# Splitting the large weight and cache loads of a decode kernel between two issuing engines, by partition halves

## The chip, the cores and the metric

The kernel runs on one core of a Trainium2 chip. The time is the device time of one execution, in microseconds (us). The kernel before took 382.42 us, the median of three runs (380.34, 382.51, 382.42).

## What is computed

One decoding step for two sequences: a layer norm, then the sum of the input, a sliding-window attention over a key and value cache, and a gated bilinear feed-forward block. All data are float32.

```python
x: (2, 1, 512); k_cache, v_cache: (2, 32, 8192, 128); wq: (512, 4096); wo: (4096, 512)
w_gate, w_up: (512, 1376); w_down: (1376, 512)

def _A_ref(x, k_cache, v_cache, wq, wo):
    W = min(4096, max(256, Sk // 4))          # 2048 of the 8192 positions
    q = (x @ wq).reshape(B, Sq, 32, 128).transpose(0, 2, 1, 3)
    k, v = k_cache[:, :, Sk - W:, :], v_cache[:, :, Sk - W:, :]
    scores = jnp.einsum("bhqd,bhkd->bhqk", q, k) * (128 ** -0.5)
    o = jnp.einsum("bhqk,bhkd->bhqd", softmax(scores), v)
    return o.transpose(0, 2, 1, 3).reshape(B, Sq, 4096) @ wo

def _B_ref(x, w_gate, w_up, w_down):
    return ((x @ w_gate) * (x @ w_up)) @ w_down

xn = layernorm(x)
out = x + _A_ref(xn, ...) + _B_ref(xn, ...)
```

There is one query row for each sequence and head, so every element of the cache window and of the weights is used a few times and then never again. The kernel has to read 159.5 MB from memory.

## The kernel before

**The stream.** The host lays all weights and the cache window out in one array, `stream`, in the order in which the kernel uses them. `blocks()` lists the loads: each is a list of fields, such as `("k", h, CK)` for the keys of head h, and lands as 128 rows, one for each partition, with the fields side by side in the row. `UNIT` is 4608 floats, 18 KB a partition: a head's keys with a piece of `wq`, or a head's values with its piece of `wo`. `STEP` is three units, 54 KB a partition, the size of one buffer.

**The loads in order.** 256 KB (the first piece of `wq`, into a tile of its own), 3072 KB (keys of head 0), 6400 KB (half of gate and up, keys of head 1), 3712 KB, 4608 KB, sixteen of 6912 KB (three units each, so by turns keys-values-keys and values-keys-values), 6400 KB, 6656 KB, 4352 KB, and then ten small ones for the last values and `w_down`. A small tile with the input `x` is loaded by ACT at the start.

**Who issues them.** `pump()` issues a load as soon as one of the `BUFS = 3` buffers of 54 KB a partition is free. It is called once at the start and then from `done()`, which a step calls when it has used a field: when the last field of a buffer is used, the buffer is given back and `pump()` puts the next load's DMA into the program at that place. All of them go to SP's queue. The wait for the buffer's last readers (the reduction of a head's products on DVE, or the projection on PE) sits on the issuing instruction, so SP waits and nothing is behind it but the next load.

**Order.** PE, DVE, ACT and SP are wrapped in `InOrder`: what the code calls on an engine runs on it in the order of the calls. Every instruction recorded through the wrapper has line 85. GpSimd (POOL) is not wrapped; a scheduler decides the order of its instructions, which are the two all-reduces over partitions of each head (L277 `mm`, the maximum, and L289 `sum`).

**A head.** `products(h)` multiplies the keys by the query on DVE (`step<-step,q`), `sums(h)` reduces them over the head dimension (`s<-step`). `weights(h)` takes the maximum (DVE `m`, POOL `mm`, ACT `nm`) and the exponentials (ACT `p`, POOL `sum`). `reciprocals(h - 1)` on DVE follows behind it. The values of a head come `LAG = 3` heads later: `pv` on PE (`o_ps`), `copy_out` on ACT (`o_sb`), `transpose` on PE (`tr`) and ACT (`oT`), `project_o` on PE (`acc`). `project_q` on PE makes the queries of later heads (`q<-step,xnb`).

Of the kernel before, what the change touches and what calls it, by code (L numbers as in the profile page):

```python
# [16 lines left out]
P = 128  # L17
# [15 lines left out]
UNIT = CK + max(CP, CO)  # L33
# [67 lines left out]
def kernel(  # L101
# [8 lines left out]
    pe, dve, act, sp = (InOrder(tc, e) for e in (nc.tensor, nc.vector, nc.scalar, nc.sync))  # L110
# [23 lines left out]
    tiles, used, left, got = {}, {}, {}, {}  # L134
# [4 lines left out]
    def pump():  # L139
        nonlocal held  # L140
        while todo:
            key, fields, at = todo[0]
            if key not in tiles:
                if key[0] == "q":
                    tiles[key] = const.tile([P, NC * DH], F32, name="wq0")
                elif held == BUFS:
                    return
                else:
                    held += 1
                    tiles[key] = steps.tile([P, STEP], F32, name="step")  # L150
                used[key] = 0
            todo.pop(0)
            c0 = used[key]
            for kind, i, w in fields:
                got[kind, i] = (tiles[key][:, used[key] : used[key] + w], key)
                used[key] += w
            c1 = used[key]
            if at is None:
                sp.dma_start(tiles[key][:FR, c0:c1], wd_rest)
            else:  # L160
                src = stream[at : at + P * (c1 - c0)].rearrange("(p i) -> p i", p=P)
                sp.dma_start(tiles[key][:, c0:c1], src)

    def done(kind, i):
        nonlocal held
        _, key = got.pop((kind, i))
        left[key] -= 1
        if left[key] == 0 and key[0] != "q":
            del tiles[key]
            held -= 1  # L170
            pump()

    pump()

    mean_w = const.tile([P, P], F32, name="mean_w")
# [353 lines left out]
```

## Time and profile before

| | |
|---|---|
| median of 3 runs | 382.42 us (380.34 to 382.51) |
| the profiled execution | 380.73 us, of which its span is 378.9 us |
| PE, busy | 260.9 us (69%) |
| DVE, busy | 293.9 us (78%) |
| ACT, busy | 63.8 us (17%) |
| POOL, busy | 25.2 us (7%) |
| moved by DMA | 159.71 MB, mean 421 GB/s over the span |
| mean granted TensorE clock | 0.797 |

A group of instructions is written as line, engine, operation, output<-input; `x31` is how often it ran. An engine followed by q (SPq, ACTq) is the queue in which it issues its DMAs. In the table of DMA queues, q1 holds the loads that SP issues and q10 those that ACT issues; both are served by the same 16 DMA engines.

### The profile page before, as it was taken

To read this page: it belongs to the slowest core of one execution; us is meant where nothing else is said; L and a number is where in the kernel's file an instruction comes from. 1 tells how busy PE (TensorE), PEld (TensorE's weight loads), DVE (VectorE), ACT (ScalarE), POOL (GpSimd) and SP (SyncE) were. 2 spreads that over 40 slices of the span, in tenths; PEclk is the share of its full clock that TensorE was granted. 3 is DMA by queue.
4 is the path that set the end of the run, shared out by engine and by line. 5 is a ranking of instruction groups with operands and counts; after the bars stand their busy time and mean duration, and the time that the engine had idled before them with its cause. 6 is when DMAs were issued, how large, how long until landed. Compare 5 with 4: busy or idle time off the path is not lost.

```text
span 378.9 us, 3009 instructions
## 1 busy us (share of the span) xinstructions
PE 260.9 (69%) x1156; PEld 90.2 (24%) x1156; DVE 293.9 (78%) x142; ACT 63.8 (17%) x264; POOL 25.2 (7%) x75
## 2 busy tenths in 40 slices
PE   3919882867838675783876668388566848719996
PEld 3502221212303221221222123122122312202442
DVE  3739892996799499589949949994994998699920
ACT  1020020102112110210111121011112112212221
POOL 0000000000000000000000000010000000000000
PEclk9968986667888796887969698667968776855999
DMA  8999999999999999999999999999999999999993
GB/s 316 463 419 435 428 444 455 403 444 461 394 444 449 403 455 409 434 461 403 444 457 391 449 455 387 461 415 432 455 414 434 455 417 433 423 427 412 421 415 143
DMA packets 4893, 159.71 MB, mean 421 GB/s; under 512 B 552, under 2 KB 688, under 8 KB 1296
## 3 DMA queue, kind: packets, MB, share of 16 engines
q1 hardware_dynamic: 4728, 159.45, 97.9%
q8 instruction: 9, 0.15, 0.2%
q10 hardware_dynamic: 152, 0.08, 0.1%
q14 instruction: 4, 0.03, 0.0%
HBM read 159.52 MB, written 0.00 MB: 421 GB/s over the span
## 4 chain that ended last, share of the span: by engine, by line
DMA 55%; DVE 24%; PE 16%; ACT 3%; issue 1%; SPq 0%; POOL 0%; DVEq 0%
DMA step<-in_stream_dram 55%; DVE s L85 12%; DVE step L85 12%; PE o_ps L85 6%; PE q L85 4%; PE acc L85 3%; PE tr L85 3%; ACT o_sb L85 1%; ACT oT L85 1%; ACT p L85 1%; DVE m L85 0%; SPq L85 0%; POOL mm L277 0%; DVE rec L85 0%; DVE o_sb L85 0%
## 5 line engine op out<-in xcount | busy, mean ns | idle before, releaser
L85 DVE TENSOR_TENSOR step<-step,q 128x4096 f32<-128x4096 f32 x31 | 136.6, 4407 | 57.2 <-DMA step<-in_stream_dram 57.2
L85 DVE TENSOR_REDUCE s<-step 128x32 f32<-128x4096 f32 x32 | 141.4, 4420 | 1.1
L85 PE MATMUL q<-step,xnb 128*128 128x512 f32 (+1 forms) x128 | 89.8, 847 | 59.4 <-DMA step<-in_stream_dram 59.2
L85 PE MATMUL o_ps<-step,p 128*8 128x512 f32 x512 | 87.7, 723 | 8.4 <-DMA step<-in_stream_dram 7.5
L85 PEld LDWEIGHTS q<-step,xnb 128*128 128x128 f32 x128 | 30.9, 265 | 113.4 <-DMA step<-in_stream_dram 56.9
L85 PE MATMUL tr<-x_t,o_sb 128*128 128x2 f32 x256 | 34.3, 256 | 25.1 <-ACT o_sb L85 24.7
L85 PE MATMUL acc<-step,oT 128*2 128x512 f32 (+1 forms) x76 | 41.1, 659 | 13.1 <-ACT oT L85 13.1
L85 PEld LDWEIGHTS tr<-x_t,o_sb 128*128 128x128 f32 x256 | 31.6, 194 | 54.7 <-ACT o_sb L85 52.1
L85 ACT COPY o_sb<-o_ps 128x512 f32<-128x512 f32 x33 | 19.2, 582 | 118.1 <-PE o_ps L85 118.1
L85 PEld LDWEIGHTS o_ps<-step,p 128*8 128x8 f32 x512 | 14.1, 96 | 75.3 <-issue 62.6
L85 ACT ACTIVATE nm<-mm 128x2 f32<-128x2 f32 x32 | 6.5, 203 | 146.0 <-POOL mm L277 146.0
L277 POOL PARTITION_ALL_REDUCE mm<-m x32 | 11.4, 355 | 288.6 <-DVE rec L85 189.4
L85 ACT ACTIVATE oT<-tr,rec 128x1 f32<-128x1 f32 x64 | 13.2, 257 | 37.4 <-PE tr L85 37.4
L85 ACT ACTIVATE p<-s,nm 128x16 f32<-128x16 f32 x64 | 19.2, 300 | 1.0
L289 POOL PARTITION_ALL_REDUCE sum<-rs x32 | 12.8, 398 | 39.5 <-ACT p L85 39.5
L85 PE MATMUL o_ps<-step,xn 128*2 128x512 f32 (+1 forms) x48 | 12.2, 558 | 0.0
L85 ACT ACTIVATION_READ_ACCUMULATOR p<-s,nm 128x1 f32 x64 | 11.9, 187 | 0.0
L85 DVE TENSOR_TENSOR o_out<-acc,x_t 128x128 f32<-128x128 f32 x1 | 0.3, 290 | 10.7 <-PE acc L85 10.7
L85 DVE TENSOR_TENSOR step<-step,tr 128x4096 f32<-128x4096 f32 x1 | 4.4, 4420 | 4.7 <-DMA step<-in_stream_dram 4.7
L85 PEld LDWEIGHTS acc<-step,oT 128*2 128x2 f32 x76 | 3.0, 82 | 16.8 <-ACT oT L85 16.8
L85 DVE TENSOR_REDUCE m<-s 128x2 f32<-128x32 f32 x32 | 5.9, 186 | 1.1
L85 PE MATMUL q<-xnb,mean_w 128*128 128x256 f32 x16 | 5.5, 426 | 0.0
(36 smaller groups left out, 36.4 us busy)
## 6 DMA issues: line engine op xcount, KB each, us to landing
step<-in_stream_dram SPq DMA_DIRECT2D x16, 6912.0 KB, 31.8
step<-in_stream_dram SPq DMA_DIRECT2D x2, 6400.0 KB, 31.5
step<-in_stream_dram SPq DMA_DIRECT2D x1, 6656.0 KB, 29.2
step<-in_stream_dram SPq DMA_DIRECT2D x1, 4608.0 KB, 26.3
step<-in_stream_dram SPq DMA_DIRECT2D x2, 2304.0 KB, 13.5
step<-in_stream_dram SPq DMA_DIRECT2D x1, 4352.0 KB, 24.2
step<-in_stream_dram SPq DMA_DIRECT2D x1, 3712.0 KB, 34.0
step<-in_stream_dram SPq DMA_DIRECT2D x1, 3072.0 KB
```

The costliest lines, as they stand in the source:

```text
L85: made = call(*args, **kwargs)
L277: nc.gpsimd.partition_all_reduce(mm, m, P, bass_isa.ReduceOp.max)
L289: nc.gpsimd.partition_all_reduce(sum_t[h], rs, P, bass_isa.ReduceOp.add)
```

## The change

Each load whose row is 36 KB a partition or more (`2 * UNIT` floats) is given out as two DMAs of 64 partitions: SP issues the lower half, ACT the upper half, at the same place in the program. This holds for 20 loads: sixteen of 6912 KB, two of 6400 KB, one of 6656 KB and one of 4608 KB. The other loads stay as they were.

```diff
             else:
                 src = stream[at : at + P * (c1 - c0)].rearrange("(p i) -> p i", p=P)
-                sp.dma_start(tiles[key][:, c0:c1], src)
+                if c1 - c0 < 2 * UNIT:
+                    sp.dma_start(tiles[key][:, c0:c1], src)
+                else:
+                    for eng, half in ((sp, slice(0, P // 2)), (act, slice(P // 2, P))):
+                        eng.dma_start(tiles[key][half, c0:c1], src[half])
```

ACT's DMAs are in ACT's program order like its other instructions. In the built program the instructions of PE, DVE and SP stand in the order they had; ACT has 20 DMAs more; and on POOL, where the scheduler decides, the all-reduces, which went by turns `mm`, `sum`, `mm`, `sum`, now have 17 of the 32 `sum` behind the `mm` of the next head: from head 7 to head 27 in a pattern of three heads, `mm` of the first, `mm` of the second, `sum` of the first, `mm` of the third, `sum` of the second, `sum` of the third.

## The prediction

> **What bounds the kernel now.** I read the page's slices and DMA queues first, then the chain that ended last, then the busy time by stage, then the waits of SP's queue and of DVE.
>
> ```profile
> DMA  8999999999999999999999999999999999999993
> GB/s 316 463 419 435 428 444 455 403 444 461 394 444 449 403 455 409 434 461 403 444 457 391 449 455 387 461 415 432 455 414 434 455 417 433 423 427 412 421 415 143
> q1 hardware_dynamic: 4728, 159.45, 97.9%
> DMA 55%; DVE 24%; PE 16%; ACT 3%; issue 1%; SPq 0%; POOL 0%; DVEq 0%
> ```
>
> The packets of SP's loads fill 97.9% of the time of the 16 DMA engines; no slice between the first and the last falls under 387 GB/s. The kernel is a stream of loads, and compute hangs on it. By stage:
>
> ```profile
> 0.00:12.00 12.00, 4.92 (x20) 4.49 (x20) 3.25 (x11) 1.54 (x2) 0.89 (x9) 1.00 0.89 358
> 196.00:261.00 65.00, 44.46 (x180) 14.39 (x179) 53.54 (x25) 11.23 (x48) 4.52 (x12) 0.79 1.01 435
> 261.00:326.00 65.00, 44.95 (x187) 14.90 (x187) 54.93 (x25) 11.24 (x48) 4.52 (x12) 0.79 1.00 433
> 370.00:379.00 9.00, 5.24 (x86) 2.62 (x82) 0.29 (x1) 1.00 (x3) 0.00 (x0) 1.00 0.35 127
> ```
>
> The last three columns are the granted clock, the DMA share and GB/s. In the middle the share is 1.00 and the rate 433 GB/s, 27.1 for each engine; only the first 12 us and the last 9 fall short. PE (69%) and DVE (82 to 85%) have room.
>
> ```profile
> step<-in_stream_dram SPq DMA_DIRECT2D x16, 6912.0 KB, 31.8
> DVE step L85 <- DMA step<-in_stream_dram: 61.9, 12, 7.3
> SPq L85 <- DVE s L85: 289.9, 22, 24.2
> SPq L85 <- PE acc L85: 51.0, 10, 6.4
> ```
>
> A load of 6912 KB (7.08 MB) needs 7.08 / 0.433 = 16.3 us, but lands 31.8 us after its issue: it first queues 15.5 us behind the load before it. So an issue may come some 15 us later before an engine runs dry. SP is free: it waits for a buffer to be given back, by DVE's reduction (22 times) or PE's projection (10).
>
> **The sum before.** The 20 loads that are split hold 16 x 6912 + 2 x 6400 + 6656 + 4608 = 134,656 KB = 137.9 MB, at 433 GB/s 318 us. The other 21.6 MB take 50 us. That is 368; the profiled execution took 380.7 (span 378.9 and 1.8 around it), so 12 lie at the two ends. The median of the runs is 1.7 above it.
>
> **The change part by part.**
>
> *Twenty more issues on ACT.* ACT's issue of the input tile took 0.42 us; 20 x 0.42 = 8.4 us on an engine that is busy 63.8 of 378.9. Nothing, since ACT idles 118.1 us for `o_ps` and 146.0 us for `mm`. Uncovered it would be 8.4.
>
> *ACT now waits for buffers.* Behind the waiting DMA stand ACT's next operations. Where the buffer is given back by `sums(h)`, the next is `nm` of the same head, which needs that reduction anyway. Where `project_o` gives it back, the next is the following `copy_out`, whose matmuls come later on the same PE: in the steady part SP issued at 227.89, the end of that projection (226.10 + 1.75), and PE then still had a query projection and 16 value matmuls ahead of the next copy. In the first loads `nm` of head 1 stands behind a wait for the gate matmuls, 37.06 against some 38.4: 1.4 us, for exponentials that are used three heads later. I put all this at nothing; without cover, 20 waits of about 1 us, 20 us.
>
> *POOL's order.* 17 of the sums now follow the next head's `mm`, and `rec` on DVE, right behind `m`, waits for them:
>
> ```profile
> 222.36 0.19 DVE L85 TENSOR_REDUCE m<-s 128x2 f32<-128x32 f32 x1
> 222.46 0.15 DVE L85 RECIPROCAL rec<-sum 128x2 f32<-128x2 f32 x1
> 222.71 0.35 POOL L277 PARTITION_ALL_REDUCE mm<-m  x1 [7.18 <-DVE rec L85]
> ...
> 224.19 0.40 POOL L289 PARTITION_ALL_REDUCE sum<-rs  x1 [1.12 <-ACT p L85]
> 228.02 4.42 DVE L85 TENSOR_TENSOR step<-step,q 128x4096 f32<-128x4096 f32 x1 [5.41 <-DMA step<-in_stream_dram]
> ```
>
> `mm` begins 0.35 us after `m` and takes 0.35, the sum 0.40: about 1.1 us of DVE each, 17 x 1.1 = 19 us in all, some 2.2 for each pair of loads. DVE waits 5.4 us for data once in such a pair (last line), so it is absorbed: nothing. Uncovered, 19.
>
> *First loads.* ACT's half of the 6400 KB load starts beside the 256 and 3072 KB loads that the first head needs. Shared evenly, these 3.4 MB land some 7 us later than now (12.1). The second head still waits for the same total, 10 MB at 27.4 us, so I put it at nothing; bound 7.
>
> *Two half loads in place of one.* This decides. In a whole load each of the 16 engines carries 8 rows. In a half all 16 still carry rows, 4 each: the tail's load of 96 rows ended with a completion from every engine, 6 rows behind each in the packet records. So with both queues filled each engine goes by turns through a row for the lower and a row for the upper 64 partitions. What this costs hangs on what holds an engine at 27.1 GB/s. If it is the engine itself, nothing changes. If it is the way into the partitions that it writes, then 16 engines that write a lower half at once go through what 8 used to use, and each gets half. No row shows a load of 64 partitions. The floor is 0 (whole loads: 433 GB/s in every stage), the ceiling +318 us (all split bytes at half rate).
>
> The nearest rows point both ways. In the last microsecond of loading two engines were still at work, one in a load of 128 rows, one in that of 96; for 0.4 us their 2 KB rows took 124 to 178 ns where such rows take 84, and then went back to 84 to 95: two engines sharing about one engine's pace. Against it, the first two engines to reach the load of 96 rows had 84 to 91 ns. I take the sharing as the likelier, because the pace is the same at 27 GB/s for rows from 18 to 54 KB, a cap outside the single row, and the one sharing that the trace shows is near a halving. Two engines that share a way run at half when both are on the same half and at full when they alternate out of step. Where one enters d into the other's row of T, a row takes 2T - d; over all phases the mean rate is ln 2 = 0.69, which is 318 x 0.44 = +141 us. But a load counts as landed only with its slowest row, and engines that wait for a buffer start the next load together, in step, so I put it nearer the ceiling: three quarters of it, +240 us, 381 + 240 = **621 us**.
>
> [...]
>
> **The rivals.**
>
> *The halves share nothing.* Each engine writes the same bytes at its own pace, and what the ACT wait, POOL's order and the first loads add lies under 15 us of queue and 5.4 us of DVE idle: 378 to 386, most likely 381. For it: the 84 to 91 ns rows. Against: the near halving. It is the rival that is not slower. To be faster it could only fill the first 12 us, 12 x (1 - 358 / 433) = 2 us, and tail loads aren't split: under 1%.
>
> *The ACT half comes late.* The memory doesn't mind, but SP's half runs ahead and a load waits for ACT's. It decides once ACT issues more than 15 us behind SP, or if the `rec` waits (19) and ACT's holds (20) fall where DVE has no idle time: of these 39 us I leave 5 to 20 unabsorbed, 386 to 400. Against it: ACT's waits are for the same events as SP's.
>
> *The halves don't run side by side.* One queue is served first, or every pair stays in step: the ceiling, 381 + 318 = 699. This is the upper end of my own case.
>
> **How the numbers follow.** What a measurement of this kernel can tell from no change is about 1%, 378.6 to 386.2 around the median. Shared ways into the partitions, 500 to 700: 0.68, and 0.04 of it above 700. Nothing shared: 0.25, of which 0.22 within 1% and 0.03 faster by more, if some gap of the stream that I don't see closes. ACT's half late, 386 to 400: 0.07, of which a third within 1%. So slower 0.72, same 0.25, faster 0.03. The likeliest case's own range is 500 to 700. Without the case of nothing shared more than 2 in 10 would be left out, so the range reaches from 379 to 700.
>
> **What would show it.** In the profile after, the second queue (q10) holds about 69 MB and q1 about 90. If the ways are shared: GB/s near 240 to 260 in the slices of the middle with the DMA share still 9, the 6912 KB loads' halves landing 50 to 60 us after issue, DVE's wait for `step` near 300 us instead of 61.9, the chain mostly DMA. If not, the slices stay at 433 and the landing at 31.8. If ACT were the cause: SP's and ACT's halves landing at different times, and DVE's wait put down to `rec` or POOL. I am wrong in the mechanism if the time is above 386 with slices at 433 GB/s, and in the size if they lie outside 220 to 340.

## The result and the profile after

The changed kernel took 708.84 us, the median of four runs (701.06 to 722.48), against 382.47 before (the median of four runs). The longest of the four, which is also the profiled one, counts as a slow run; without it the kernel takes 1.850 times as long as before, 95% interval 1.839 to 1.862. The forecast was 621, its range 379 to 700. The direction and the mechanism came true, the size did not.

The page of the kernel after; the lines answer to those of the prediction's first fence. The profiled execution took 722.48 us, its span 720.7.

```profile
DMA  9999999999999999999999999999999999999996
GB/s 232 229 202 204 204 227 210 200 230 206 203 230 207 203 227 209 206 228 209 218 215 210 218 218 206 224 216 212 224 209 233 206 231 207 224 225 209 220 418 260
...
q1 hardware_dynamic: 3448, 90.51, 54.3%
q10 hardware_dynamic: 1752, 69.02, 44.8%
...
another core or an unknown queue 48%; DVE 37%; DMA 12%; POOL 2%; issue 1%; SPq 0%; DVEq 0%; ACT 0%; ACTq 0%; PE 0%; POOLq 0%
```

The DMA engines are as busy as before in every slice, and up to the last two slices, where whole loads come again, they move half as much: no engine stands idle, each row takes twice as long (54 KB: 2.045 us before, 4.1 after, medians of the packet records). The second queue holds the 69 MB of ACT's halves. A kernel on one core has no other core to wait for: the chain's 48% "unknown queue" stands where the 55% of the loads stood before, which the profile no longer puts down to one queue. By stage (the last three columns are the granted clock, the DMA share and GB/s):

```profile
0.00:12.00 12.00, 4.93 (x20) 4.49 (x20) 3.25 (x11) 1.54 (x2) 1.13 (x11) 1.00 0.90 238
...
200.00:300.00 100.00, 33.26 (x124) 10.90 (x124) 45.56 (x20) 8.47 (x37) 3.29 (x9) 0.64 1.00 213
300.00:400.00 100.00, 38.84 (x146) 11.80 (x146) 36.57 (x16) 8.57 (x35) 3.34 (x9) 0.62 1.00 214
...
500.00:600.00 100.00, 34.92 (x146) 11.76 (x146) 36.58 (x16) 8.57 (x35) 3.34 (x9) 0.64 1.01 220
```

The middle runs at 213 to 220 GB/s, about half of 433, where the prediction had 240 to 260 for this case and called itself wrong in size outside 220 to 340. The loads' issues on the page (number, size, us to landing), then the waits (us in all, times, longest) of the engines and of SP's queue:

```profile
step<-in_stream_dram SPq DMA_DIRECT2D x16, 3456.0 KB, 81.8
step<-in_stream_dram ACTq DMA_DIRECT2D x16, 3456.0 KB, 49.2
```

```profile
DVE step L85 <- DMA step<-in_stream_dram: 383.5, 22, 32.0
...
DVE rec L85 <- POOL sum L293: 15.7, 17, 0.9
```

```profile
SPq L85 <- DVE s L85: 622.1, 22, 41.9
```

DVE does nearly the same work, 296.6 us against 293.9; its wait for data grew from 61.9 to 383.5 us, and that growth of 322 us is nearly all of the 342 by which the two profiled executions differ. ACT's halves land earlier than SP's, probably because SP's queue also holds the whole loads of the start. And the whole loads suffer too. The first multiplication of keys, which needs whole loads only (256 and 3072 KB), started at 12.16 us before; the timeline after:

```profile
34.78 4.42 DVE L85 TENSOR_TENSOR step<-step,tr 128x4096 f32<-128x4096 f32 x1 [27.30 <-DMA step<-in_stream_dram]
```

### The profile page after: what moved, and what is told of

It is laid out like the page before. It is cut to its first block, busy times and chain, and to the rows that moved or that the text cites. A ratio compares the mean times of both kernels' runs of the same rounds, so it can differ in the third digit from the quotient of the medians.

```text
span 720.7 us, 3090 instructions
## 1 busy us (share of the span) xinstructions
PE 273.5 (38%) x1156; PEld 94.0 (13%) x1156; DVE 296.6 (41%) x142; ACT 64.2 (9%) x264; POOL 24.8 (3%) x75
## 4 chain that ended last, share of the span: by engine, by line
another core or an unknown queue 48%; DVE 37%; DMA 12%; POOL 2%; issue 1%; SPq 0%; DVEq 0%; ACT 0%; ACTq 0%; PE 0%; POOLq 0%
DVE s L85 18%; DVE step L85 18%; DMA step<-in_stream_dram 9%; DMA step<-in_wd_rest_dram 3%; POOL sum L293 1%; POOL mm L281 1%; DVE m L85 1%; DVE rec L85 1%; SPq L85 0%; DVE o_sb L85 0%; DVEq L85 0%; ACT o_sb L85 0%; ACTq L85 0%; PE acc L85 0%
## 5 line engine op out<-in xcount | busy, mean ns | idle before, releaser
L85 PE MATMUL q<-step,xnb 128*128 128x512 f32 (+1 forms) x128 | 100.1, 934 | 376.5 <-DMA step<-in_stream_dram 376.5
L85 PE MATMUL o_ps<-step,p 128*8 128x512 f32 x512 | 85.6, 725 | 25.7 <-DMA step<-in_stream_dram 25.0
L85 PEld LDWEIGHTS q<-step,xnb 128*128 128x128 f32 x128 | 34.3, 294 | 435.0 <-issue 377.3
L281 POOL PARTITION_ALL_REDUCE mm<-m x32 | 11.4, 356 | 651.5 <-DVE m L85 508.9
L293 POOL PARTITION_ALL_REDUCE sum<-rs x32 | 14.0, 438 | 17.9 <-ACT p L85 17.9
L85 DVE RECIPROCAL rec<-sum 128x2 f32<-128x2 f32 x32 | 5.1, 160 | 15.7 <-POOL sum L293 15.7
## 6 DMA issues: line engine op xcount, KB each, us to landing
step<-in_stream_dram SPq DMA_DIRECT2D x3, 2304.0 KB, 15.7
```

The costliest lines, as they stand in the source:

```text
L85: made = call(*args, **kwargs)
L281: nc.gpsimd.partition_all_reduce(mm, m, P, bass_isa.ReduceOp.max)
L293: nc.gpsimd.partition_all_reduce(sum_t[h], rs, P, bass_isa.ReduceOp.add)
```

## Experiments

The theory: what holds an engine at 27 GB/s lies, at least in part, where it writes; with 64 neighbouring partitions as the target, 16 engines share what 8 used. The rivals: the interleaving of two queues costs; ACT's waits cost; the reads cost; the number of rows in a load costs. The split by columns (also with POOL's order held) and the one by every second partition have four or five runs each, the other kernels one run each; the kernel before took 380.7 to 385.1 us beside them.

**Split by columns.** Two issuers, two queues and all of ACT's waits, but 128 partitions in each half.

```diff
-for eng, half in ((sp, slice(0, P // 2)), (act, slice(P // 2, P))):
-    eng.dma_start(tiles[key][half, c0:c1], src[half])
+mid = (c1 - c0) // 2
+for eng, part in ((sp, slice(0, mid)), (act, slice(mid, c1 - c0))):
+    eng.dma_start(tiles[key][:, c0:c1][:, part], src[:, part])
```

> The 20 large loads are split between SP and ACT as in the changed kernel, but by columns: each half has all 128 partitions and half of each row (27 KB of 54 KB). Both queues, ACT's waits and POOL's order stay. If the 64 partitions of a half are what costs (shared ways into the partitions): the slices back at about 433 GB/s, 6912 KB loads landing some 32 us after issue, 378 to 388 us. If two queues that interleave, or ACT holding its half, are what costs: near 700 us, at the least above 420.

387.79 us, 1.9% over the kernel before (interval 1.2 to 2.6%). Its stages:

```profile
163.00:261.00 98.00, 67.03 (x270) 23.44 (x270) 81.56 (x35) 16.08 (x71) 5.89 (x16) 0.80 1.00 430
261.00:326.00 65.00, 43.96 (x180) 15.72 (x180) 53.96 (x25) 10.90 (x48) 4.41 (x12) 0.82 1.01 431
```

The rate is back at 430 GB/s, with the same two queues and the same waits. Queues and ACT explain some 7 us, not 326.

**One queue.** The halves by partitions again, but both issued by SP (`act` replaced by `sp` in the loop).

> Both halves of 64 partitions are issued by SP, the upper behind the lower; ACT issues nothing. Shared ways into the partitions: while a lower half is served all 16 engines write lower partitions, so the 137.9 MB go at half of 433 GB/s, 381 + 318 = 699 us, 690 to 710, and the whole loads keep their pace (first multiplication of keys near 12 us, not 34.8). If the interleaving of two queues costs: 378 to 390 us.

734.09 us, even slower; the middle at 207 GB/s:

```profile
300.00:600.00 300.00, 98.08 (x381) 31.89 (x380) 114.55 (x50) 22.95 (x97) 9.04 (x24) 0.62 1.00 207
```

With ACT out of it altogether the halving is there: two queues aren't needed. In the packet records, the profile's times of single DMA packets, a row of 54 KB takes 4.33 us (median) here, 4.1 in the changed kernel, 2.045 before. The first multiplication of keys starts at 15.07 us, near the 12 that I expected if whole loads keep their pace. The 699 us that I had as a ceiling isn't one: 137.9 MB / 0.207 are 666 us where I put 637.

**Every second partition.** The same halves of 64 rows, SP the even partitions, ACT the odd ones.

```diff
-((sp, slice(0, P // 2)), (act, slice(P // 2, P)))
+((sp, slice(0, P, 2)), (act, slice(1, P, 2)))
```

> Halves of 64 partitions, SP the even ones, ACT the odd ones, read and written so that every row lands where it belongs. If touching partitions all over the 128 is what frees the load: 433 GB/s in the slices, 6912 KB loads near 32 us to landing, and only the side costs of two issuers are left: 381 to 392 us. If the gain of the misplaced rows came from the reads: 500 us or more.

383.21 us, 0.9% over before (0.5 to 1.3%). Its stages, and its issues:

```profile
57.00:163.00 106.00, 72.48 (x287) 23.90 (x286) 87.44 (x40) 17.45 (x76) 7.00 (x19) 0.77 1.00 432
163.00:326.00 163.00, 113.29 (x450) 38.22 (x450) 136.33 (x59) 27.30 (x117) 10.35 (x28) 0.79 1.00 432
```

```profile
step<-in_stream_dram SPq DMA_DIRECT2D x16, 3456.0 KB, 31.5
step<-in_stream_dram ACTq DMA_DIRECT2D x16, 3456.0 KB, 24.8
```

Two queues, 64 rows in a load, 4 rows for each engine (in the changed kernel's packet records every half ends with 16 completions), all as in the changed kernel; only which partitions a half covers differs, and nearly the whole cost is gone. So neither the number of rows nor the queues make up the 326 us. Two more runs separate the two ends of the transfer.

```diff
# strided_dst
-eng.dma_start(tiles[key][half, c0:c1], src[half])
+eng.dma_start(tiles[key][n::2, c0:c1], src[half])
# strided_src
+eng.dma_start(tiles[key][half, c0:c1], src[n::2])
```

> The halves are read from memory as in the changed kernel (rows 0 to 63 by SP, 64 to 127 by ACT) but written to every second partition (even by SP, odd by ACT), so each half touches partitions all over the 128; the rows land in other partitions than they should. If the place written is what is shared: the time changes, to 381 to 400 us if what counts is how many partitions' ways one load touches, in between if engines still meet on neighbouring partitions. If the reads (where the rows lie in memory) are what is shared: 700 to 725 us, as before.

> The counterpart: written to partitions 0 to 63 and 64 to 127 as in the changed kernel, but read from every second row of the source (even rows by SP, odd by ACT); the rows land in other partitions than they should. If the place written is what is shared: 695 to 725 us, as the changed kernel. If the reads are: clearly below 690.

386.01 us with the target spread and the reads as in the changed kernel, its middle at 432 and 433 GB/s; 700.15 us with the reads spread and the target as in the changed kernel, its middle at 216 and 222. The kernel before took 385.10 beside both. It is the place written. Why 64 neighbouring partitions halve the rate (207 to 222 GB/s in the middle stages, on one queue and on two) and every second one does not (432 and 433) no run here shows.

**How large, and beside what.** Two kernels that split fewer loads.

```diff
-if c1 - c0 < 2 * UNIT:
+if c1 - c0 < STEP:                                           # only_54
+if c1 - c0 < STEP or key[1] not in (8, 9, 10, 11):           # four
```

> Only the sixteen loads of 6912 KB are split by partitions between SP and ACT; the others are whole. The split bytes are 113.2 MB, 262 us at 433 GB/s. Shared ways at half rate: 381 + 262 = 643 us, 635 to 655, and the first multiplication of keys back at 12 us. If engines that are not in step share less: well below 640.

> Only four of the sixteen 6912 KB loads in the middle of the run are split by partitions. At half rate each costs 16.3 us more: 381 + 65 = 446 us, 440 to 452. Where engines don't stand in step, as when only the 6912 KB loads were split (14.7 us a load): 425 to 440 us. If the cost is one of the whole stream and not of the split loads: far from both.

Both missed what plain halving asks, on opposite sides. With the sixteen loads of 54 KB a partition alone: 616.94 us, (616.9 - 380.9) / 16 = 14.8 us a load, less than a full halving's 16.3; its middle stages run at 233 and 260 GB/s, and the first multiplication starts at 11.92 us again. With four loads: 475.95 us, (476.0 - 380.7) / 4 = 23.8 us a load, much more. Stages of the kernel with four:

```profile
57.00:90.00 33.00, 18.39 (x70) 6.02 (x71) 25.81 (x10) 4.67 (x21) 1.90 (x5) 0.73 1.00 432
90.00:165.00 75.00, 23.80 (x94) 7.45 (x90) 28.66 (x15) 6.19 (x28) 2.56 (x7) 0.61 1.01 228
165.00:250.00 85.00, 29.97 (x114) 9.13 (x109) 27.38 (x12) 7.05 (x30) 2.61 (x7) 0.62 1.02 218
...
280.00:340.00 60.00, 41.78 (x160) 13.58 (x164) 47.32 (x24) 10.24 (x45) 4.36 (x12) 0.79 1.00 431
```

In the page's slices the slow stretch lasts from about 100 to 272 us, and its slowest slices have 168 GB/s, below the half. Four halved loads need only 4 x 32.7 = 131 us. In the packet records rows of whole loads on SP's queue alternate there with rows of ACT's halves, which take up to 6.6 us. A whole load queued beside a half pays as well: 362 rows of 54 KB on SP's queue took over 2.7 us, and only 256 rows there belong to halves, so at least 106 rows of whole loads were slowed. At half the four loads would cost 65 us; the other 30 fall to these whole loads and to rows of halves that were slower than half, in shares that aren't worked out.

**Do the engines that share stand in step?** That was my reason for a cost between 141 and 318 us. The packet records give the rows under way on each queue at a moment, and how long these rows took in the end (times on the records' own clock):

```
kernel             at us   rows on q1, median us   rows on q10, median us
changed kernel     303.0   16   4.09                0   -
changed kernel     315.0    8   4.09                8   4.15
only_54            304.5    8   3.14                8   3.14
strided            318.0   16   2.04                0   -
strided            310.5    8   2.05                8   2.05
```

That the engines take the two queues by turns, as the prediction had it, the changed kernel's records show: no row on q1 and 16 on q10 at 299.0 us, 16 and none at 303.0, 1 and 15 at 307.0. With 8 rows on each half the changed kernel is as slow as with 16 on one, and the strided one as fast with 16 on one as with 8 on each: it isn't a lower and an upper block with a rate for each, since 8 and 8 would then be quick. Nor is it quick at any other moment: of the changed kernel's 2048 rows of 54 KB none took under 3.87 us. Smaller groups of engines that share a way and keep to the same half would fit this; the records name no engine, so it isn't shown. In the kernel with only the 54 KB loads split, the same mix goes 30% faster at that moment (3.82 us is the median of all its rows of 54 KB): the mix alone doesn't set the pace, and how engines stand to one another may. Four kernels tried to set them apart, by small loads that are to make some engines lose a turn, and a fifth (16 rows) is their control. That a small load goes to as many engines as it has rows is an estimate from the records of the kernels before and after: loads of 64, 96 and 128 rows end with 16 completions, each of the two stores of 4 rows with 4. Which engines these are, and whether two small loads go to the same ones, isn't shown. Ahead of the first half load:

```diff
# flip8, flip16: 8 or 16 rows of 2 KB
+lead = stream[0 : 8 * 512].rearrange("(p i) -> p i", p=8)
+sp.dma_start(shift[P // 2 : P // 2 + 4 * 8 - 3 : 4, :], lead)
# phase8: 8 rows of 27 KB on each queue, only the 54 KB loads split
# flip_4: 4, 8 and 12 rows of 1 KB; flip_2: 2, 4, 6, 8, 10, 12 and 14 rows
```

> As the kernel that splits only the 6912 KB loads, and just ahead of the first of them two small loads of 8 rows of 27 KB, one on each queue, into a tile that nothing reads: 8 rows go to 8 of the 16 engines, so these come one row of 54 KB late against the other 8. If the halving is two engines of a pair standing in step on the same half, and the step is kept once it is set, half of the engines now write lower rows while the others write upper ones: rows near 2.0 to 2.6 us instead of 4.1, 385 to 470 us. If a load of 64 partitions is held to half whatever the other engines do, or the engines fall back into step: 640 to 660 us.

> The changed kernel with one small load more: just ahead of SP's first half of a 6912 KB load, SP loads 8 rows of 2 KB into a tile that nothing reads. 8 rows go to 8 of the 16 engines, which so spend one of SP's turns on a row of some 0.1 us and go on with an upper row while the other 8 read a lower one. If engines share by pairs, one from each 8, and are slow because both stand on the same half: rows of 55 KB at 2.1 to 2.6 us instead of 4.1, GB/s above 330 from the fifth load on, 425 to 500 us. If the halving doesn't hang on who reads what at the same time, or the pairs lie within one group of 8: 700 to 725 us.

> The same small load with 16 rows of 2 KB, one for every engine: all engines lose the same turn and stay as they stood to each other. In every theory that speaks of how engines stand to each other: 695 to 725 us, as the changed kernel. If it comes out near the kernel with 8 rows, the small load itself does something that I don't understand.

> [...]

> [...]

None came out faster where the theory of step wanted it. 8 rows of 27 KB: 661.07 us, slower than the 616.94 without them, at 208 to 221 GB/s in every slice of the middle. 8 rows of 2 KB: 712.83; 16 rows: 676.96, the control and yet the faster one; 4, 8 and 12 rows: 725.02; 2 to 14 rows: 720.08. Kernels that differ only in such small loads differ by 44 us (phase8 and only_54) and 36 (flip16 and flip8), where the changed kernel's own runs spread over 21. So something about the order counts beside the partitions, but these are single runs, and the control, which was to leave the engines as they stood, came out furthest from the changed kernel: the theory of step is not shown. In phase8 the two small loads passed some 40 us apart (from 38.6 and from 79.5 us in the packet records), so whether they set the engines apart as meant isn't known either. Which engine takes which rows of a half, and whether engines that share come back together, stays open.

**Other ranges of partitions.** SP 32 to 95 in one DMA, ACT 0 to 31 and 96 to 127 in two.

```diff
+for eng, rows in ((sp, slice(32, 96)), (act, slice(0, 32)), (act, slice(96, P))):
+    eng.dma_start(tiles[key][rows, c0:c1], src[rows])
```

> SP loads partitions 32 to 95 in one DMA, ACT the outer ones in two DMAs of 32. [...] If any run of 64 or fewer neighbouring partitions is halved: 690 to 730 us. If the number of rows in one load is what counts: above 700 us.

748.43 us, the slowest of all, over the 690 to 730 of a halving for every run of 64 or fewer neighbouring partitions. Above 700 was to speak for the number of rows in a load, but the kernel with loads of 64 rows over every second partition took 383.21. Rows of 54 KB took from 2.2 to 7.0 us. The 64 partitions in the middle gained nothing here, with the two loads of 32 under way beside them. It doesn't tell how the middle load would go alone.

**POOL's order.** The column split with the all-reduces held as before, `mm`, `sum`, by turns.

```diff
+pool = InOrder(tc, nc.gpsimd)
-nc.gpsimd.partition_all_reduce(...)
+pool.partition_all_reduce(...)
```

> The split by columns, with POOL's all-reduces held in the order of the kernel before (mm, sum, mm, sum). If the 1.9% of the column split come from sums that stand behind the next head's mm: 0 to 0.5% over the kernel before, 381 to 384 us. If they come from the two queues and the landing order of the loads: 1.5 to 2.5% again, 386 to 391 us.

386.4 us, 1.7% over before (1.0 to 2.3%), against 1.9% without it. The intervals overlap, so the order is at most a small part of what the column split costs.

## Why the prediction was wrong in size

**What bounds the kernel: right.** Every version that kept 430 GB/s stayed within 2% of the kernel before; every one that lost it was far longer.

**Two half loads in place of one: the right mechanism, mis-sized.** The step that failed is "three quarters of it, +240 us". Measured are +326 us (708.84 - 382.47). I had weighed engines out of step (a mean of 0.69) against engines in step (half), and the stream ran at 213 to 220 GB/s throughout, the in-step end. Of the engines out of step, whose weight brought the sum down from the ceiling, the rows show nothing: by the prediction's 2T - d they would spread from 2.05 to 4.09 us, and the shortest took 3.88. Of my reasons, that a load lands with its slowest row fits the trace: the multiplication at 309.25 us, which had waited for its load, began 11.1 us behind the first completion of the two halves and 0.94 behind the last. That engines which wait for a buffer start together is neither shown nor refuted; why the rows all stay at the slow end is open.

**The ceiling of +318 us: not a ceiling.** It counted the split bytes alone. The whole loads of 3072 and 3712 KB, 6.95 MB, stand beside ACT's first half and go at about half as well: 16 us more. With both, (137.9 + 6.95) / 0.2145 + 14.65 / 0.433 + 12 = 675 + 34 + 12 = 721 us, against the profiled 722.5. This takes the rate that was measured, so it tells where the time lies and forecasts nothing. At exactly half of 433 the same bytes give 381 + 318 + 16 = 715; the other three runs, 701 to 711 us, lie under that. That whole loads beside halves pay is shown by the four split loads and by the rows of the first loads (below); the 16 us are worked out. A half on one queue even falls to 207 GB/s.

**First loads: wrong.** I had the first head's keys 7 us later; they came 22.6 us later (34.78 against 12.16). Sharing evenly between the queues was too kind: the rows of 24 KB also slowed, from 0.91 to 1.56 us (medians of the packet records), and the second queue's rows of 50 KB between them did as well, from 1.89 to 4.0. The second head, which I had left where it was, came late too, at 51.01 us against 27.48.

**POOL's order: right.** 17 waits of `rec`, foreseen at 1.1 us each, 19 in all; measured 17 and 15.7 us. The lines answer to those of before; L281 and L293 are L277 and L289 of the kernel before:

```profile
294.03 0.19 DVE L85 TENSOR_REDUCE m<-s 128x2 f32<-128x32 f32 x1
...
294.38 0.35 POOL L281 PARTITION_ALL_REDUCE mm<-m  x1 [8.78 <-DVE m L85]
294.64 0.47 POOL L293 PARTITION_ALL_REDUCE sum<-rs  x1
...
295.15 0.17 DVE L85 RECIPROCAL rec<-sum 128x2 f32<-128x2 f32 x1 [0.93 <-POOL sum L293]
...
309.25 4.42 DVE L85 TENSOR_TENSOR step<-step,q 128x4096 f32<-128x4096 f32 x1 [13.94 <-DMA step<-in_stream_dram]
```

The wait of 0.93 us is there, and data are 13.94 us away behind it. Putting it right in the column split left the time within its interval, so "nothing" holds as far as these runs can tell.

**ACT's issues and waits: nearly right.** I put them at nothing; together with the second queue they cost 0.9% (every second partition) to 1.9% (columns). Which of issue, wait or landing order that is wasn't tried.

**The rivals.** *Nothing shared* fell: the 84 to 91 ns rows that spoke for it misled me, and why those two engines weren't slowed remains unexplained. *The ACT half comes late* fell: ACT's halves land first, and one queue alone is as slow. *The halves don't run side by side* was nearest, priced too low.

## What to carry to other kernels

When a kernel keeps the DMA engines busy throughout, as this one does (share 1.00 at 433 GB/s), look at which partitions a load writes before looking at who issues it: loads over partitions 0 to 63 and 64 to 127 ran at 213 to 220 GB/s here, loads over every second partition at 432, over all 128 with half the columns at 430. A bound must include what stands beside the changed work: loads that weren't touched slowed as well, and my worst case left them out. And a DMA share of 1.00 says only that the engines are busy, here at 433 GB/s as well as at 213; read GB/s beside it.

## What the runs showed that I had not expected

Half loads on one queue are slower (734.09 us in a single run, 207 GB/s) than on two (708.84, about 215). Four split loads cost 23.8 us each, sixteen 14.8. A load of 16 rows of 2 KB, once, ahead of the first split load of 6912 KB, came with a run 32 us shorter than the changed kernel's median, a single run that I can't explain. No version was faster than the kernel before.
